# 32-column tiles and attention in fewer, larger visits, in a fused Linformer attention and hard-swish MLP

## The chip, the cores and the metric

One Trainium2 chip, one of its cores. The metric is the device time of one execution in microseconds (us). Every quoted time is a median of single executions; their range stands beside it where it matters.

## The reference

Eight batches of eight heads, 1024 tokens, head size 64. Keys and values are projected along the sequence to 64 rows (E and F), so that attention is over 64 keys. Its output is the input of an MLP with a hard-swish gate.

```python
k_proj = einsum('ks,bhsd->bhkd', E, k);  v_proj = einsum('ks,bhsd->bhkd', F, v)
scores = q @ k_proj.T / sqrt(64)
attn = softmax(scores)                      # over the 64 projected keys
x = (attn @ v_proj)  -> (8 * 1024, 512)     # heads side by side
h = x @ w_in                                # 512 -> 2048
out = (h * clip(h + 3, 0, 6) / 6) @ w_out   # 2048 -> 512, float32
```

## The kernel before

The MLP of a batch is two halves of 512 tokens. A half has 16 *first groups* (a row block of h: 4 blocks of the 512 inputs summed in one PSUM bank, then the gate on ScalarE and VectorE) and 4 *output groups* (16 blocks summed in one bank, then a copy and a write to DRAM). The output groups of one half run between the first groups of the next, one after every four. Attention of the next batch is done at those places in *visits*: TensorE leaves the MLP for a few matmuls of another tile shape. A change of shape leaves a gap between matmuls, called a *drain* here. Two pools of four PSUM banks each, `mm` and `at`, go round in order; a bank comes free when ScalarE or VectorE has read it out (its *eviction*).

Parts that the change touches (cuts marked):

```python
    ps_mm = ctx.enter_context(tc.tile_pool(name="ps_mm", bufs=4, space=bass.MemoryType.PSUM))
    ps_at = ctx.enter_context(tc.tile_pool(name="ps_at", bufs=4, space=bass.MemoryType.PSUM))
    width = [P // 2]                      # 64 columns of the array per matmul

    def in_columns(ps, stationary, moving, **flags):
        for lo in range(0, stationary.shape[-1], width[0]):
            nc.tensor.matmul(ps[lo:lo + width[0]], stationary[:, lo:lo + width[0]], moving, **flags)
    # ... cut ...
        def all_sums(self, alloc):        # denominators of all heads: 128x32 tiles
            tiles = [alloc() for _ in range(2)]
            for h in range(H):
                j, a, c = h // 2, h % 2, h % 4
                nc.tensor.matmul(tiles[h // 4][32 * c:32 * c + 32].rearrange("p (r n) -> p r n", r=2),
                                 halves.rearrange("p t i -> p (t i)"), self.aT[j][:, :, a, :],
                                 start=True, stop=True)
            return tiles

        def spread(self, den):            # reciprocals to DRAM and back, one row to 64 partitions
            few = att.tile([P, 2, TOK], f32, tag="few", name="few", bufs=1)
            inverse(few, den)             # two logarithms, one exponential on ScalarE
            rows = dram.tile([H, NB, TOK], f32, tag="rows", name="rows")
            nc.sync.dma_start(out=rows..., in_=few[::16])
            self.recs = [rec_tile() for _ in range(KO)]
            for h in range(H):
                nc.sync.dma_start(out=self.recs[h // 2]..., in_=rows[h:h + 1]...to_broadcast([D, NB * TOK]))
    # ... cut: visit(n), the four visits of batches 1 and 2, each head pair's sums made with 64x64 tiles ...
            if b == 1:                    # batch 2 is attended here, by head pair
                n -= SB
                if n < 3:
                    return lambda: second.visit(n, third), nothing
                return nothing, lambda: second.visit(n, third)()
            if b + 1 < B:                 # batches 3 to 7: several visits, sums and first values together
                # ... cut: two special scores visits and a projection of batch 2 ...
                if n == 0:
                    return nothing, lambda: second.some_scores((1, 2, 3), ((pmm, pmm), (pat, pat), (pat, pmm)), third)
                if n == 2:
                    return second.sums_and_values, nothing
                if n == 5:
                    return second.first_products, nothing
                if n == 6:
                    return lambda: second.last_values(third), nothing
    # ... cut ...
        for t in range(NB):
            if b == 1 and t == 1:
                qT_dma[3] = q_transposed(3)     # transposing DMA, SyncE's queue
```

The softmax here doesn't subtract the row's maximum and nothing guards it: scores larger than these inputs give would overflow.

## Time and profile before

| | before |
|---|---|
| time, median of 6 executions | 507.19 us (507.05 to 507.40) |
| span in the profile | 505.5 us |
| TensorE busy, mean granted clock | 99%, 1.0 |
| matmuls; runs of one tile shape | 4858; 92 |

TensorE is the bound, so what counts is any time in which it does not start the next *set* of tiles (the matmuls that share the array side by side: two of 64 columns or four of 32). I read that from the *starts* of matmuls in the timeline, because the ends are modelled; the prediction below shows the lines. In them `few` are the logarithms and reciprocals of the sums, `rows` their copy in DRAM, `rec` the broadcast reciprocals, `xT` the output of the attention, `r` and `g` the gate. Two more page lines of before are of use later, the products of the values with the reciprocals (they wait for ScalarE, never for a DMA) and the queue of instruction fetches (count, MB, share):

```profile
q8 instruction: 38, 0.62, 0.5%
L264 DVE TENSOR_TENSOR xT<-at,rec 128x512 bf16<-128x512 f32 x42 | 26.5, 681 | 6.5 <-ACT rec L184 6.5
```

### The profile page before, as it was taken

How to read it: one execution, taken by the hardware profiler on the slowest of the kernel's cores; microseconds unless marked ns; L12 is line 12 of the kernel's file. 1: busy time of each engine (PE TensorE's matmuls, PEld its weight loads, DVE VectorE, ACT ScalarE, POOL GpSimd, SP SyncE). 2: the span in 40 equal slices, each digit the busy share in tenths (PEclk: the TensorE clock that was granted, in tenths of full speed). 3: DMA queues.
4: the chain of work that ended last, by engine and by line, in shares of the span. 5: the costliest groups of instructions: out<-in, count | busy, mean ns of one | idle time of the engine just before them, and what ended most of it. 6: DMA issues, size and time to landing. Idle time of an engine off the chain costs nothing.

```text
span 505.5 us, 11242 instructions
## 1 busy us (share of the span) xinstructions
PE 498.9 (99%) x4858; PEld 259.5 (51%) x4858; DVE 245.1 (48%) x384; ACT 256.1 (51%) x438; POOL 38.7 (8%) x58
## 2 busy tenths in 40 slices
PE   8999999999999999999999999999999999999997
PEld 4554554554454555545554555545555555555554
DVE  3572736865733564536635455533752446334420
ACT  3757466566565444653555544654455544344431
POOL 8620020020020020020001000000000000000000
PEclk9999999999999999999999999999999999999999
DMA  9999979799299999699416992248110361101112
GB/s 168 198 205 208 200 131 231 142 155 202 73 151 194 230 169 190 137 154 249 123 43 118 205 249 69 61 100 209 43 43 29 82 164 43 39 26 43 43 43 84
DMA packets 78074, 66.30 MB, mean 131 GB/s; under 512 B 36216, under 2 KB 67192, under 8 KB 78024
## 3 DMA queue, kind: packets, MB, share of 16 engines
q0 software_dynamic: 32480, 29.36, 37.4%
q1 hardware_dynamic: 45320, 35.89, 27.7%
q8 instruction: 38, 0.62, 0.5%
q10 hardware_dynamic: 224, 0.33, 0.2%
q14 instruction: 12, 0.10, 0.1%
HBM read 69.73 MB, written 16.94 MB: 171 GB/s over the span
## 4 chain that ended last, share of the span: by engine, by line
PE 85%; DMA 12%; POOL 2%; ACT 1%; issue 0%; DVE 0%; ACTq 0%; POOLq 0%
PE mm L172 79%; DMA q<-in_q_dram 6%; DMA w_in_sb<-in_moe_w_in_dram 2%; PE at L172 2%; DMA v<-in_v_dram 2%; DMA qT<-q 2%; PE at L251 1%; PE at L233 1%; PE mm L251 1%; POOL q L106 1%; PE mm L271 1%; POOL k L110 1%; ACT aT L242 0%; PE mm L233 0%; POOL v L110 0%
## 5 line engine op out<-in xcount | busy, mean ns | idle before, releaser
L512 DVE SCALAR_TENSOR_TENSOR g<-r,mm 128x512 bf16<-128x512 f32 x256 | 173.5, 686 | 178.7 <-ACT r L511 177.9
L172 PE MATMUL mm<-w_out_sb,g 128*64 128x512 bf16 (+2 forms) x2080 | 235.0, 376 | 0.2 <-DVE g L512 0.2
L172 PE MATMUL mm<-xT,w_in_sb 128*64 128x512 bf16 x2048 | 231.5, 379 | 0.3
L511 ACT ACTIVATE r<-mm 128x512 f32<-128x512 f32 x256 | 152.2, 599 | 74.5 <-PE mm L172 73.5
L172 PEld LDWEIGHTS <-w_in_sb 128*64 128x64 bf16 x2048 | 117.2, 110 | 104.0 <-issue 0.8
L172 PEld LDWEIGHTS <-g 128*64 128x64 bf16 x2080 | 116.2, 110 | 105.5 <-issue 7.0
L546 ACT COPY o_sb<-mm 128x512 f32<-128x512 f32 x55 | 32.2, 586 | 126.7 <-PE mm L172 126.7
L264 DVE TENSOR_TENSOR xT<-at,rec 128x512 bf16<-128x512 f32 x42 | 26.5, 681 | 6.5 <-ACT rec L184 6.5
L242 ACT ACTIVATE aT<-at 128x512 bf16<-128x512 f32 x38 | 20.2, 615 | 9.1 <-PE at L233 9.1
L208 DVE CAST kp<-at 64x512 bf16<-64x512 f32 x12 | 7.7, 677 | 15.9 <-PE at L172 15.9
L223 POOL COPY mark<-qT 1x1 bf16<-1x1 bf16 x4 | 0.7, 176 | 165.0 <-DMA qT<-q 165.0
L242 ACT ACTIVATE aT<-mm 128x512 bf16<-128x512 f32 x18 | 10.3, 613 | 3.9 <-PE mm L233 3.9
L546 DVE COPY o_sb<-mm 128x512 f32<-128x512 f32 x8 | 5.5, 687 | 13.8 <-PE mm L172 13.8
L172 PE MATMUL at<-v,f_t 128*64 128x512 bf16 x48 | 11.4, 381 | 0.3 <-DMA v<-in_v_dram 0.3
L172 PE MATMUL at<-k,e_t 128*64 128x512 bf16 x48 | 11.6, 382 | 0.0
L264 DVE TENSOR_TENSOR xT<-mm,rec 128x512 bf16<-128x512 f32 x14 | 9.0, 685 | 4.3 <-PE mm L251 4.3
L184 ACT ACTIVATE rec<-rec 128x1024 f32<-128x1024 f32 x10 | 10.6, 1060 | 0.3
L178 ACT ACTIVATE rec<-mm 128x512 f32<-128x512 f32 x10 | 5.5, 595 | 7.9 <-PE mm L251 5.4
L178 ACT ACTIVATE few<-mm 128x512 f32<-128x512 f32 x10 | 5.4, 594 | 7.4 <-PE mm L271 7.4
L93 PE MATMUL mm<-ones 128*128 128x512 bf16 x18 | 7.4, 549 | 1.5 <-DVE halves L84 1.5
L172 PEld LDWEIGHTS <-e_t 128*64 128x64 bf16 x56 | 5.7, 110 | 6.0 <-issue 1.8
L211 DVE CAST vp<-at 64x512 bf16<-64x512 f32 x12 | 8.3, 694 | 0.4
(73 smaller groups left out, 155.0 us busy)
## 6 DMA issues: line engine op xcount, KB each, us to landing
out_dram<-o_sb SPq DMA_DIRECT2D x63, 256.0 KB, 3.0
rec<-rows SPq DMA_DIRECT2D x40, 256.0 KB, 6.5
k<-in_k_dram POOLq DMA_DIRECT2D x7, 1024.0 KB, 15.0
v<-in_v_dram POOLq DMA_DIRECT2D x7, 1024.0 KB, 20.7
q<-in_q_dram POOLq DMA_DIRECT2D x7, 1024.0 KB, 10.0
w_out_sb<-in_moe_w_out_dram POOLq DMA_DIRECT2D x4, 512.0 KB, 16.0
w_in_sb<-in_moe_w_in_dram POOLq DMA_DIRECT2D x5, 256.0 KB, 9.7
k<-in_k_dram POOLq DMA_DIRECT2D x4, 256.0 KB, 5.5
```

The costliest lines, as they stand in the source:

```text
L93: nc.tensor.matmul(ps, ones[:, :P], ones, start=True, stop=True)
L172: nc.tensor.matmul(ps[lo:lo + width[0]], stationary[:, lo:lo + width[0]], moving, **flags)
L178: nc.scalar.activation(rec[:, i], den, AF.Ln)
L184: nc.scalar.activation(flat, flat, AF.Exp, scale=-1.0)
L208: nc.vector.tensor_copy(self.kp[:, :, a, :], self.ps[:KP].rearrange("p (h d) -> p h d", d=D))
L211: nc.vector.tensor_copy(self.vp[a * KP:(a + 1) * KP], self.ps[KP:].rearrange("p (h d) -> p h d", d=D))
L242: nc.scalar.activation(self.aT[j][:, r].rearrange("p a n -> p (a n)"), tiles[r], AF.Exp, scale=scale)
L251: nc.tensor.matmul(tiles[t][c:c + D].rearrange("p (r n) -> p r n", r=2), stationary(r, 2 * j + a), self.aT[j][r:r + KP, :, a, :], start=Tr ...
L264: nc.vector.tensor_mul(self.xT[:, j, t, :], av[t], rec[:, t])
L511: nc.scalar.activation(r, h_ps, AF.Relu, bias=0.5, scale=1.0 / 6.0)
L512: nc.vector.scalar_tensor_tensor(g[:, fo, :], r, 1.0, h_ps, op0=ALU.min, op1=ALU.mult)
L546: (copy or nc.scalar.copy)(o_sb, o_ps)
```

## The change

Its intent: let the big matmuls use the same tile shape, 128x32, as the sums of the softmax, so that the sums no longer drain TensorE; and collect the attention of a batch into few visits that use all eight banks, to change shape less often. Batch 2, until now attended by head pair with its sums kept on the chip, gets the same treatment: its reciprocals go out to DRAM and are broadcast back. The diff cut to its core:

```diff
+    width[0] = P // 4                     # from batch 1 on: four matmuls instead of two
+        def all_banks(self, make, take):
+            tiles = [make(j, *two) for j, two in enumerate(((pmm, pmm), (pat, pat), (pat, pat), (pmm, pmm)))]
+            for j in (0, 3, 1, 2):        # two head pairs evicted now, two spread over later groups
+                take(j, tiles[j], later.append if j in (1, 2) else lambda f: f())
 # ... cut ...
-            if b == 1: ... return lambda: second.visit(n, third), nothing   # and the rest of visits()
+        inside, behind_it = {}, {}
+        if b == 1:
+            behind_it = {4: second.all_scores, 5: second.sums_spread}
+            inside = {6: second.first_values, 7: second.last_values}
+        elif b == 2:
+            inside = {0: second.projected}
+            behind_it = {1: second.all_scores, 2: second.sums_spread, 4: third.projected, 6: second.all_values}
+        elif b + 1 < B:
+            behind_it = {0: second.all_scores, 1: second.sums_spread, 5: second.all_values}
+            if third:
+                behind_it[3] = third.projected
 # ... cut ...
-                rows = second_group(*behind[0], fo // SB, nc.vector.tensor_copy if b == 1 else None)
+                rows = second_group(*behind[0], fo // SB,
+                                    nc.vector.tensor_copy if (b, n) in ((1, 4), (2, 1)) or (b > 2 and n == 0) else None)
```

`inside` runs in the middle of an output group, `behind_it` after it. The numbers are output groups of the half behind, 0 to 7 within a batch. The transposing DMA of batch 3's queries stays where it was. Cut, but part of the change: batch 1's first scores visit comes four blocks (8 matmuls) later, the projections move, and the queries of batches 5 to 7 are loaded after their keys and values and no longer before them.

More of the change, by code (lines that the diff above doesn't have):

```diff
@@ L223, in turn @@
                 nc.gpsimd.tensor_copy(mark, last)
-                load_kqv(self.b + 1, "kvq" if self.b in (1, 3) else "qkv")
+                load_kqv(self.b + 1, "qkv" if self.b == 2 else "kvq")
         def scores(self, j, *allocs):
@@ L237, in scores, with exps @@
             return tiles
-        def exps(self, j, tiles):
-            self.aT[j] = att.tile([P, 2, 2, HT], bf16, tag="aT", name="aT", bufs=KO + 1)
+        def exps(self, j, tiles, when=lambda f: f()):
+            self.aT[j] = aT = att.tile([P, 2, 2, HT], bf16, tag="aT", name="aT", bufs=KO + 1)
             for r in range(2):
-                nc.scalar.activation(self.aT[j][:, r].rearrange("p a n -> p (a n)"), tiles[r],
-                                     AF.Exp, scale=scale)
+                when(lambda r=r: nc.scalar.activation(aT[:, r].rearrange("p a n -> p (a n)"), tiles[r],
+                                                      AF.Exp, scale=scale))
         def quads(self, stationary, j, allocs):
@@ L260, in values, with scaled @@
             return self.quads(lambda r, h: self.vp[r:r + KP, h, :], j, allocs)
-        def scaled(self, j, av, rec):
+        def scaled(self, j, av, rec, when=lambda f: f()):
             for t in range(NB):
-                nc.vector.tensor_mul(self.xT[:, j, t, :], av[t], rec[:, t])
+                when(lambda t=t: nc.vector.tensor_mul(self.xT[:, j, t, :], av[t], rec[:, t]))
         def all_sums(self, alloc):
@@ L285, in spread, with projected, all_scores, all_values @@
                                   in_=rows[h:h + 1].rearrange("h t n -> h (t n)").to_broadcast([D, NB * TOK]))
-        def projected(self, alloc=pat):
-            self.project(alloc)
+        def projected(self):
+            self.project(pat)
             self.keys_out()
-            rest = [lambda: self.values_out(0), lambda: None, lambda: None, lambda: self.values_out(1)]
-            if alloc == pmm:
-                for r in rest:
-                    r()
-                rest = []
-            later.extend([self.turn] + rest)
-        def some_scores(self, js, allocs, following=None):
-            tiles = [self.scores(j, *alloc) for j, alloc in zip(js, allocs)]
-            for j, two in zip(js, tiles):
-                self.exps(j, two)
-            if following:
-                following.projected()
-        def sums_and_values(self):
-            den = self.all_sums(pmm)
+            later.extend([self.turn, lambda: self.values_out(0), lambda: None,
+                          lambda: self.values_out(1)])
+        def all_banks(self, make, take):
+            tiles = [make(j, *two) for j, two in enumerate(((pmm, pmm), (pat, pat), (pat, pat), (pmm, pmm)))]
+            for j in (0, 3, 1, 2):
+                take(j, tiles[j], later.append if j in (1, 2) else lambda f: f())
+        def all_scores(self):
+            self.all_banks(self.scores, self.exps)
+        def all_values(self):
+            self.all_banks(self.values, lambda j, av, when: self.scaled(j, av, self.recs[j], when))
+        def sums_spread(self):
+            self.spread(self.all_sums(pmm))
+        def first_values(self):
             self.av = [self.values(j, pat, pat) for j in range(2)]
-            self.spread(den)
         def first_products(self):
@@ L314, in first_products, with last_values, visit @@
                 self.scaled(j, self.av[j], self.recs[j])
-        def last_values(self, following):
-            av = [self.values(2, pmm, pmm), self.values(3, pat, pat)]
-            if following:
-                following.some_scores((0,), ((pat, pat),))
+        def last_values(self):
+            av = [self.values(2, pmm, pmm), self.values(3, pmm, pat)]
             for i in range(2):
                 self.scaled(2 + i, av[i], self.recs[2 + i])
-        def visit(self, n, following):
+        def visit(self, n):
             if n == 0:
-                self.some_scores((2, 0, 1), ((pmm, pmm), (pat, pat), (pat, pat)))
+                js = 2, 0, 1
+                tiles = [self.scores(j, *two) for j, two in zip(js, ((pmm, pmm), (pat, pat), (pat, pat)))]
+                for j, two in zip(js, tiles):
+                    self.exps(j, two)
                 return lambda: None
@@ L348, in visit @@
             self.scaled(2, early, self.rec)
-            if following:
-                following.project(pat)
-                later.extend([following.turn] + [lambda a=a: following.values_out(a) for a in range(2)])
-            def rest():
-                self.scaled(3, av, rec)
-                if following:
-                    following.keys_out()
-            return rest
+            return lambda: self.scaled(3, av, rec)
     class First:
@@ L622 @@
             pop()
-            if i == 0:
-                rest.append(second.visit(c, None))
+            if i == (c == 0):
+                rest.append(second.visit(c))
             elif i == 2 or c == SB - 1:
@@ L637 @@
         third = Attention(b + 2) if b + 2 < B else None
-        def visits(b, n):
-            def nothing():
-                pass
-            if b == 1:
-                n -= SB
-                if n < 3:
-                    return lambda: second.visit(n, third), nothing
-                return nothing, lambda: second.visit(n, third)()
-            if b + 1 < B:
-                six = (pmm, pmm), (pat, pat), (pat, pat)
-                if (b, n) == (2, 0):
-                    return lambda: second.some_scores((2, 0, 1), six), nothing
-                if (b, n) == (2, 1):
-                    return lambda: second.some_scores((3,), six[1:2]), nothing
-                if (b, n) == (2, 3):
-                    return lambda: third.projected(pmm), nothing
-                if n == 0:
-                    return nothing, lambda: second.some_scores(
-                        (1, 2, 3), ((pmm, pmm), (pat, pat), (pat, pmm)), third)
-                if n == 2:
-                    return second.sums_and_values, nothing
-                if n == 5:
-                    return second.first_products, nothing
-                if n == 6:
-                    return lambda: second.last_values(third), nothing
-            return nothing, nothing
+        inside, behind_it = {}, {}
[9 more added lines that the diff above has]
+                behind_it[3] = third.projected
         for t in range(NB):
@@ L683 @@
                     continue
-                inside, after = visits(b, t * SB + fo // SB)
-                rows = second_group(*behind[0], fo // SB, nc.vector.tensor_copy if b == 1 else None)
+                n = t * SB + fo // SB
+                if (b, n) == (1, 7):
+                    second.first_products()
+                rows = second_group(*behind[0], fo // SB,
+                                    nc.vector.tensor_copy if (b, n) in ((1, 4), (2, 1)) or (b > 2 and n == 0) else None)
                 next(rows)
                 next(rows)
-                rest = inside()
+                if n in inside:
+                    inside[n]()
                 whole(rows)
-                after()
-                if rest:
-                    rest()
+                if n in behind_it:
+                    behind_it[n]()
             behind = [(b, t, g)]
```

## The prediction

> **What bounds the kernel now.** I read the page first, then the timeline of TensorE in stretches of batches 2 to 6, then the timelines of all engines around the attention visits, then the DMA issues of SyncE. The page says that TensorE is the bound: busy 99%, its clock at full speed in every slice, and the chain that ended last is almost wholly its matmuls.
>
> ```profile
> PE 498.9 (99%) x4858; PEld 259.5 (51%) x4858; DVE 245.1 (48%) x384; ACT 256.1 (51%) x438; POOL 38.7 (8%) x58
> PEclk9999999999999999999999999999999999999999
> ```
>
> A busy engine can still lose time between matmuls, so I looked at starts. In the timeline (start us, duration us, engine, line) 32 matmuls of 64 columns, that is 16 pairs, take 207.48 to 210.93:
>
> ```profile
> 207.48 3.62 PE L172 MATMUL mm<-w_out_sb,g 128*64 128x512 bf16 x32
> 210.93 3.62 PE L172 MATMUL mm<-xT,w_in_sb 128*64 128x512 bf16 x32
> 214.38 1.89 PE L172 MATMUL mm<-w_out_sb,g 128*64 128x512 bf16 x16
> 216.21 0.61 PE L271 MATMUL mm<-aT,halves 128*32 128x512 bf16 x8
> 216.75 0.63 PE L251 MATMUL at<-aT,vp 64*64 64x512 bf16 x8
> 217.31 1.05 PE L172 MATMUL mm<-w_out_sb,g 128*64 128x512 bf16 x8
> ```
>
> That is 3.45/16 = 0.216 us a pair, against 512 columns at 2.4 GHz = 0.213. The stream is within 1.3% of its floor. What is left is **changes of tile shape**: the 8 pairs from 214.38 take 1.83 us instead of 1.73, the 8 sums of 128x32 (two sets of four) 0.54 instead of 0.43, the 8 of 64x64 0.56 instead of 0.43: about 0.12 us at each change. Before has, by its instruction order, 92 runs of one shape.
>
> **What the Trainium skill says.** (1) "TensorEngine Tiling (Array Packing)", Key Properties: changing the tiling mode drains TensorE, changing the tile within a mode does not. The trace agrees: 0.12 us at each change. (2) The same page, PSUM Bottleneck: tiling speeds up TensorE but not the emptying of PSUM, which may become the bound. The stall at 382 below is such a case. (3) "TensorE: Matmul & The Clock Gate", Back-to-back issue gap: a warm matmul of 512 columns costs 512/2.4 plus some 2.5 ns. The trace's 0.216 agrees; I take the 2.5 ns to be per set of tiles side by side, as pairs show. (4) The same page, Part 1: after about 3.4 us of idleness the clock falls to half. The only stop shown here is at the very end of the trace, so no stretch of the kernel before tests it.
>
> **The change, part by part.**
>
> *32-column tiles.* Some 1870 sets of two become sets of four: twice the matmuls and weight loads in the same 0.216 us, so 8 instructions in 216 ns. The scores already do more: 24 matmuls and 24 loads from 106.07 to 106.85. And the sums show that four tiles of 128 rows stream at once: their two sets take 0.54 with the change of shape in it. So the stream itself: 0 us. Its use is that the sums (128x32) no longer change the shape.
>
> ```profile
> 106.07 0.41 PE L233 MATMUL mm<-qT,kT 64*64 64x256 bf16 x8
> 106.31 0.61 PE L233 MATMUL at<-qT,kT 64*64 64x256 bf16 x16
> 106.85 1.92 PE L172 MATMUL mm<-w_out_sb,g 128*64 128x512 bf16 x16
> ```
>
> *Fewer visits.* The instruction order of after has 74 runs of one shape: 18 changes fewer x 0.12 = **-2.2 us**. Batch 2's sums by head, 4 sets of 0.216 where the new form needs 2: **-0.4**. Stalls that go: 0.27 before the first scores at 68.80 (a transposing DMA; the visit moves half a microsecond or more later), some 0.3 at 139, and 0.66 after the scores of the last attended batch at 382, where three evictions on ScalarE precede what TensorE waits for: **-1.2**.
>
> *All eight banks in one visit.* The four banks of mm and four of at go round in order, so a visit that takes four mm tiles takes the bank of the output just summed, too, and the groups after it meet its evictions. The stall at 382 of before gives the delays:
>
> ```profile
> 381.49 0.41 PE L233 MATMUL mm<-qT,kT 64*64 64x256 bf16 x8
> 381.60 0.58 ACT L546 COPY o_sb<-mm 128x512 f32<-128x512 f32 x1 [2.86 <-PE mm L172]
> 382.26 3.97 PE L172 MATMUL mm<-xT,w_in_sb 128*64 128x512 bf16 x32
> 384.95 2.14 ACT L511 ACTIVATE r<-mm 128x512 f32<-128x512 f32 x4
> 385.65 2.48 DVE L512 SCALAR_TENSOR_TENSOR g<-r,mm 128x512 bf16<-128x512 f32 x4 [6.19 <-ACT r L511]
> 386.39 3.64 PE L172 MATMUL mm<-w_out_sb,g 128*64 128x512 bf16 x32 [0.16 <-DVE g L512]
> ```
>
> The copy of an output starts 0.11 after the next matmul; from a group's activation to the release of its bank is 386.39 - 384.95 = 1.44.
> Scores visit, from its first matmul S: three heads' pairs end at S+0.68; the eighth bank is that of the output, whose copy (now VectorE, 0.69) ends at S+0.11+0.69+0.05 = S+0.85: 0.17 of stall, six visits = **+1.0**. The later evictions fit: the exponentials are spread over the following groups.
> Sums visit, from its first matmul E: no drain, so the copy starts at E+0.21; then two logarithms (0.54 each) and an exponential of 1.06 end near E+2.85; the first activation of the next groups comes only then, its bank is free at E+2.82+1.44 = E+4.26. The output group that wants this bank is due at E+0.44+16x0.216 = E+3.90: 0.36, six visits = **+2.2**. In before half of an output group lay behind the sums and hid this.
> Values visit: the first product (0.69) starts 0.45 after the visit's start and frees the next group's bank at 1.19, due at 1.05; with 0.06 for the eighth bank 0.19, five visits = **+1.0**.
>
> *Batch 2's sums through DRAM.* This is the term that decides. By the same rates batch 1 in after has its sums at 115.7, their exponential done near 118.6. The reciprocals then go out and come back through SyncE's queue, behind the transposing DMA of batch 3's queries, which is unchanged:
>
> ```profile
> 110.73 13.55 SPq L160 DMA_TRANSPOSE qT<-q  x1
> 124.37 8.00 SPq L547 DMA_DIRECT2D out_dram<-o_sb  x4
> 157.13 0.72 SPq L281 DMA_DIRECT2D rows<-few  x1
> 160.50 4.96 SPq L284 DMA_DIRECT2D rec<-rows  x8
> ```
>
> It holds SyncE until 124.3 because the loads of batch 3's keys and values fill the DMA engines until about 123.6. Then two output writes (0.6, 0.4) stand before the rows: issued at 125.3, landed behind the outputs at about 128.2. Eight broadcasts follow: by before's semaphore records the first lands 3.7 us after its issue (160.50, 164.16), then one each 1.14 us (the last at 172.0). So 131.9, 133.0, ... 139.9. Two make one pair of heads. The products then stand at: first pair 133.05 to 134.4, second from 135.35, third from 137.6, fourth from 139.9 to 140.6 for its first half.
> TensorE comes to the last values of batch 2 at 129.3; their eighth tile needs the at bank of the first product: waits till 133.8. Half an output group, 1.73, to 135.85. Batch 2's first two groups need xT of pair 2 (136.0), pair 3 (138.35), pair 4 (140.65) and end at 141.1. Without waiting they end at 133.3: **+7.8 us**. TensorE being the bound, nothing later gives it back. A pause of some 4 us may drop the clock (the skill's fourth point): half speed for one to two microseconds of what follows, an expected **+0.7**.
>
> Sum: 507.3 - 2.2 - 0.4 - 1.2 + 1.0 + 2.2 + 1.0 + 7.8 + 0.7 = **516.2**; I say 516.
>
> **The rivals.** *A: the reciprocals come in time.* If the queries' transposing DMA lets SyncE go at about its usual 4.9 us (as at 92.6, 266.9 and 326.9 in before), the rows go out at 118.6 and the last broadcast lands near 132: a stall of at most 1 us, total 508 to 509. Against it: nothing in the change touches that DMA or the loads it competes with. *B: the new visits don't stall,* because the schedule was laid out for it (copies on VectorE, exponentials deferred): then the recurring 4.2 us vanish, 512 with the batch 2 stall, 504 with A as well. Against it: the bank order and the stall at 382, which the same arithmetic reproduces. *C: 32-column tiles stream worse* (loads of weights not hidden, or the sequencer at its limit): each 5 ns a set costs 9 us. Against it the scores and the sums above; for it, that no long stream of such sets is in the trace. *D: the clock falls at the pause and stays low* for its whole window or more: 1 to 2 us on top, 518.
>
> **Range and chances.** A at about 15%, B in part 20%, C 8%, D 25% of the cases. 80% range 507 to 519. Faster by over 2% (below 497.2) needs a gain that no term holds: 3%. Slower by over 2% (above 517.5) comes with C, D or a longer wait in batch 2: 24%. The rest, 73%, within 2%.
>
> **What would show the steps right or wrong.** A pause of TensorE of 3 to 5 us near 129, and two smaller ones before 141, ended by VectorE's products, which themselves waited on DMA rec<-rows; the rows issued after 124 and behind the queries' transposing DMA. Steady sets of four each 0.216 us. After each sums visit from batch 2 on, the next output group started about 0.4 us late, released by VectorE g; after scores and values visits 0.2. 74 runs of one shape, 0.12 us at each change. The prediction is wrong if the rows go out before 120, if sets of four are spaced by more than 0.218 us, or if the first values of batch 2 find their reciprocals landed.

## The result, and the profile after

| | before | after |
|---|---|---|
| time, median of 6 | 507.19 us | 518.73 us (517.14 to 519.56) |
| span in the profile | 505.5 us | 516.9 us |
| mean granted clock | 1.0 | 0.993 |
| runs of one tile shape | 92 | 74 |

The ratio of fast runs is 1.0223 (95% interval 1.0209 to 1.0238). It is, here and below, the mean time of one kernel's fast runs over the mean of the other's in the same rounds, so it is not quite the ratio of the medians quoted. The kernel is slower by just over 2%.

These page lines answer to those of before: TensorE's busy share fell to 97%; one slice of the clock row (the eleventh, 129 to 142 us) is a 7; the products now wait 7.5 us for `rec<-rows`, a DMA, and matmuls wait 6.4 us for a product; instruction fetches rose from 38 to 67.

```profile
PE 501.5 (97%) x8562; PEld 269.2 (52%) x8562; DVE 245.8 (48%) x387; ACT 243.6 (47%) x426; POOL 38.7 (7%) x58
PEclk9999999999799999999999999999999999999999
q8 instruction: 67, 1.10, 0.9%
L264 DVE TENSOR_TENSOR xT<-at,rec 128x512 bf16<-128x512 f32 x31 | 20.8, 684 | 13.3 <-DMA rec<-rows 7.5
L251 PE MATMUL at<-aT,vp 64*64 64x512 bf16 x62 | 5.5, 385 | 6.4 <-DVE xT L264 6.4
```

**The stage between batches 1 and 2.** The table of fixed windows says where the loss is. First before, then after; columns are the window, its length, busy time and instruction count of each engine, then the granted clock, the DMA share and GB/s:

```profile
127.00:146.00 19.00, 18.99 (x196) 9.60 (x194) 12.32 (x19) 12.41 (x22) 2.80 (x4) 1.00 0.39 70
```

```profile
127.00:146.00 19.00, 12.25 (x175) 5.12 (x170) 9.01 (x14) 4.06 (x7) 0.00 (x0) 0.82 0.79 178
```

TensorE is idle for 6.75 us of these 19, and the clock averages 0.82. The timeline of SyncE in after tells why (start, duration, issuing instruction):

```profile
112.93 13.35 SPq L160 DMA_TRANSPOSE qT<-q  x1
126.38 1.94 SPq L541 DMA_DIRECT2D out_dram<-o_sb  x2
128.41 0.72 SPq L281 DMA_DIRECT2D rows<-few  x1
131.52 4.96 SPq L284 DMA_DIRECT2D rec<-rows  x8
```

The transposing DMA of batch 3's queries holds SyncE from 112.93 to 126.28. Two output writes, then the reciprocals stand behind it. By the semaphore records the eight broadcasts land from 135.09 to 142.96. And the timeline of TensorE and VectorE there:

```profile
130.59 0.62 PE L251 MATMUL mm<-aT,vp 64*64 64x512 bf16 x6
136.86 1.29 DVE L264 TENSOR_TENSOR xT<-at,rec 128x512 bf16<-128x512 f32 x2 [6.55 <-DMA rec<-rows]
137.60 0.64 PE L251 MATMUL at<-aT,vp 64*64 64x512 bf16 x2 [6.39 <-DVE xT L264]
138.17 3.61 PE L172 MATMUL mm<-w_out_sb,g 128*32 128x512 bf16 x32
141.39 1.29 DVE L264 TENSOR_TENSOR xT<-mm,rec 128x512 bf16<-128x512 f32 x2 [0.98 <-DMA rec<-rows]
142.13 4.03 PE L172 MATMUL mm<-xT,w_in_sb 128*32 128x512 bf16 x64 [0.36 <-DVE xT L264]
143.08 0.69 DVE L264 TENSOR_TENSOR xT<-mm,rec 128x512 bf16<-128x512 f32 x1 [0.40 <-DMA rec<-rows]
145.98 1.91 PE L172 MATMUL mm<-w_out_sb,g 128*32 128x512 bf16 x32
```

The values visit stops after six of its eight matmuls, because the seventh needs a bank that a product must empty, and the product needs its reciprocals. It waits 6.39 us. The next eight sets (32 matmuls) then start 427 ns apart, not 216: the record of the granted clock stands at 0.5 from 136.1 to 142.9. The stage's excess over an undisturbed one is 9.6 us: 7.0 in the visit and 2.6 from there to the end of batch 2's first four groups at 145.98. The half clock makes eight sets 1.7 us longer, but that is no loss of its own: they stand ahead of a wait. The matmul at 142.13 could not start before the product of 141.39, nor the seventh set of these groups (143.82 in the trace) before the product of 143.08, and both products waited for broadcasts, the last of which landed at 142.96. So the last landing sets the end of the stage; the experiment with a busy pause comes back to this.

**The recurring visits.** A sums visit of after, on all engines:

```profile
280.00 0.60 PE L271 MATMUL mm<-aT,halves 128*32 128x512 bf16 x8
280.43 3.63 PE L172 MATMUL mm<-xT,w_in_sb 128*32 128x512 bf16 x64
280.70 1.09 ACT L178 ACTIVATE few<-mm 128x512 f32<-128x512 f32 x2
281.83 1.06 ACT L184 ACTIVATE few<-few 128x1024 f32<-128x1024 f32 x1
282.79 2.04 ACT L505 ACTIVATE r<-mm 128x512 f32<-128x512 f32 x4
284.14 1.05 PE L172 MATMUL mm<-w_out_sb,g 128*32 128x512 bf16 x16
```

The sums take 0.43 us, exactly two sets: no drain. But the four first groups behind them take 284.14 - 280.43 = 3.71 us instead of 3.45, since their first gate starts only at 282.79, behind the logarithms and the exponential. So 0.26 us are lost. Scores and values visits show 0.20 us of excess beyond their shape changes.

**Outside all this**, the first wait for batch 1's values near 55 us was 1.3 us longer in this execution, in a part of the program that the change leaves as it was; over the traces of all kernels here that wait varies from nothing to 1.8 us. And from the end of the last copy to the end of the program it takes 3.23 us instead of 2.65.

### The profile page after: what moved, and what is told of

Same layout as the page of the kernel before. It is cut to its first block, busy times and chain, and to the rows that moved or that the text cites. A ratio compares the mean times of both kernels' runs of the same rounds, so it can differ in the third digit from the quotient of the medians.

```text
span 516.9 us, 18651 instructions
## 1 busy us (share of the span) xinstructions
PE 501.5 (97%) x8562; PEld 269.2 (52%) x8562; DVE 245.8 (48%) x387; ACT 243.6 (47%) x426; POOL 38.7 (7%) x58
## 4 chain that ended last, share of the span: by engine, by line
PE 82%; DMA 11%; ACT 2%; issue 2%; POOL 1%; DVE 1%; SPq 1%; ACTq 0%; DVEq 0%; POOLq 0%
PE mm L172 76%; DMA v<-in_v_dram 7%; PE at L172 2%; DMA w_in_sb<-in_moe_w_in_dram 2%; DMA rec<-rows 1%; ACT few L178 1%; PE mm L233 1%; PE mm L251 1%; PE at L251 1%; DVE g L506 1%; PE at L233 1%; ACT r L505 1%; DMA rows<-few 1%; POOL q L106 1%; SPq L284 1%
## 5 line engine op out<-in xcount | busy, mean ns | idle before, releaser
L172 PE MATMUL mm<-w_out_sb,g 128*32 128x512 bf16 (+3 forms) x3904 | 235.1, 378 | 0.4
L172 PE MATMUL mm<-xT,w_in_sb 128*32 128x512 bf16 (+1 forms) x3840 | 232.8, 380 | 0.6 <-DVE xT L264 0.4
L172 PEld LDWEIGHTS <-g 128*32 128x32 bf16 (+1 forms) x3904 | 122.1, 98 | 102.1 <-issue 6.7
L172 PEld LDWEIGHTS <-w_in_sb 128*32 128x32 bf16 (+1 forms) x3840 | 119.2, 98 | 102.9 <-issue 4.9
L264 DVE TENSOR_TENSOR xT<-at,rec 128x512 bf16<-128x512 f32 x31 | 20.8, 684 | 13.3 <-DMA rec<-rows 7.5
L264 DVE TENSOR_TENSOR xT<-mm,rec 128x512 bf16<-128x512 f32 x25 | 15.7, 684 | 14.2 <-PE mm L251 12.9
L172 PE MATMUL at<-v,f_t 128*32 128x512 bf16 (+1 forms) x104 | 13.2, 379 | 1.6 <-DMA v<-in_v_dram 1.6
L172 PE MATMUL at<-k,e_t 128*32 128x512 bf16 (+1 forms) x104 | 13.5, 379 | 0.0
L172 PEld LDWEIGHTS <-e_t 128*32 128x32 bf16 (+1 forms) x104 | 6.2, 98 | 6.9 <-issue 2.1
L233 PEld LDWEIGHTS <-kT 64*64 64x64 bf16 x224 | 5.7, 106 | 4.2 <-issue 4.1
## 6 DMA issues: line engine op xcount, KB each, us to landing
w_out_sb<-in_moe_w_out_dram POOLq DMA_DIRECT2D x4, 512.0 KB, 15.9
```

The costliest lines, as they stand in the source:

```text
L233: nc.tensor.matmul(tiles[r][t * KP:(t + 1) * KP, a * HT:(a + 1) * HT], self.kT[r * D:(r + 1) * D, 2 * j + a, :], qT[r * D:(r + 1) * D, j, ...
L264: when(lambda t=t: nc.vector.tensor_mul(self.xT[:, j, t, :], av[t], rec[:, t]))
```

## The experiments

The theory after reading the traces: (1) the greater part of the loss (9.6 of 11.4 us between the two traces) is batch 2's reciprocals, late because they queue behind a transposing DMA on SyncE; (2) the new visits return what the saved shape changes bring; (3) sets of four cost nothing in the stream. Rivals: 32-column tiles are slow in themselves; or the detour through DRAM is slow even when it is issued in time.

### Batch 3's queries after batch 2's reciprocals

After, with one DMA issued later:

```diff
-            if b == 1 and t == 1:
-                qT_dma[3] = q_transposed(3)
 # ...
                 if n in behind_it:
                     behind_it[n]()
+                if (b, n) == (1, 5):
+                    qT_dma[3] = q_transposed(3)
```

> The changed kernel with one thing moved: the transposing DMA of batch 3's queries is issued behind the eight broadcasts of batch 2's reciprocals and not before them. Theory (SyncE's queue, held by that DMA, is what makes the reciprocals late): the rows go out near 120 and not at 128.4, the last broadcast lands some 6 us earlier, the long pause in the last values visit of batch 2 (6.4 us in the changed kernel) is gone, some 3 to 4 us of waiting for the last pairs' reciprocals before batch 2's first group stay, the clock stays at full speed: 512 to 514 us. Rival (the DMA engines' bandwidth under the loads of batch 3 is the limit, whatever the order): the broadcasts land as late as before, 517 us or more.

Measured: 511.62 us (510.88 to 512.02), just under the range that I expected; ratio to before 1.0082 (1.0069 to 1.0095). SyncE in this run:

```profile
118.51 0.71 SPq L281 DMA_DIRECT2D rows<-few  x1
123.02 4.96 SPq L284 DMA_DIRECT2D rec<-rows  x8
128.15 9.14 SPq L160 DMA_TRANSPOSE qT<-q  x1
```

and TensorE:

```profile
129.16 0.62 PE L251 MATMUL mm<-aT,vp 64*64 64x512 bf16 x6
129.53 0.40 PE L251 MATMUL at<-aT,vp 64*64 64x512 bf16 x2
129.86 1.91 PE L172 MATMUL mm<-w_out_sb,g 128*32 128x512 bf16 x32
133.35 1.48 PE L172 MATMUL mm<-xT,w_in_sb 128*32 128x512 bf16 x24 [1.58 <-DVE xT L264]
136.71 2.34 PE L172 MATMUL mm<-xT,w_in_sb 128*32 128x512 bf16 x40 [1.88 <-DVE xT L264]
```

The values visit no longer stops, and the clock stays at full speed. The medians differ by 7.1 us for moving one DMA. Between the two traces it is 6.7: 5.7 in this stage (an excess of 3.9 and not 9.6) and 1.4 from the early wait, which was short here, less 0.4 of a longer tail. So the order on SyncE's queue is shown to be the cause of 5.7 to 7.1 us of the loss, half of it or more. The last broadcast lands 7.1 us earlier (135.88 against 142.96), so it was not the load of the DMA engines alone. The two waits left, some 3.8 us by starts, come from the broadcasts themselves, which land one every 1.3 us up to 135.88: even issued in time, the way through DRAM takes from 118.5 to 135.9.

### Batch 2 by head pair, as before

After, with batch 2's four visits of the kernel before and the projection behind the fourth (cut: VectorE again copies all outputs of that stretch, as in before):

```diff
-            behind_it = {4: second.all_scores, 5: second.sums_spread}
-            inside = {6: second.first_values, 7: second.last_values}
+            inside = {4 + i: lambda i=i, a=second: a.visit(i) for i in range(3)}
+            behind_it = {7: lambda a=second, f=third: a.visit(3, f)()}
```

> The changed kernel with batch 2 attended as in the kernel before (four visits, sums by head, no trip through DRAM, keys and values of batch 3 projected behind the fourth). Theory: the pause and the half clock, together 9.6 us in the trace, go; two more changes of tile shape and 0.4 of sums come back, 0.5 of stalls in batch 2's scores and sums visits go: 509.0 to 509.8 us. Rival (the recurring visits or the 32-column stream are the greater part of the loss): 513 or more.

Measured: 507.68 us, ratio 1.0013 (0.9998 to 1.0027): lower than I expected, in part because there was no early wait for values in its trace (1.8 us less than in after). With batch 2 taken back, 11 of the 11.5 us are gone. Everything else in the change, 32 columns, fewer visits and their new stalls, comes out at nothing within 0.3%.

### 32 columns alone, on the kernel before

```diff
+    width[0] = P // 4
     second = Attention(2)
```

> The kernel before with 32-column tiles from batch 1 on and nothing else. It has 88 runs of one tile shape where before has 92. Theory (a set of four streams as a pair does, a change of shape costs 0.12 us): 0.5 us faster, 506.7, ratio 0.999. Rival (weights or instructions of four tiles are not hidden): each 1 ns a set costs 1.9 us, so over 508 us.

Measured: 509.85 us (508.56 to 512.56), ratio 1.0052 (1.0033 to 1.0071). My theory said 506.7 and was wrong, yet the stream was as I said: steady sets of four start 216 ns apart. The loss sits in one place, the projection of batch 5:

```profile
202.56 0.39 PE L172 MATMUL at<-k,e_t 128*32 128x512 bf16 x2
204.78 0.39 PE L172 MATMUL at<-v,f_t 128*32 128x512 bf16 x2 [1.82 <-DMA v<-in_v_dram]
```

The values landed at 204.73 here, at 201.53 in before, where they were due at 202.3: before had a margin of 0.8 us. Some 2.0 us are lost to that wait and 0.6 in the tail (3.21 us against 2.65). The load was issued 3.3 us later, too (184.18 against 180.91), and so it was in the eased pair below (183.73 with 32 columns, 180.81 with 64): the shift comes with the tiles, but what makes it is not shown.

### 64 columns in the changed kernel

After without `width[0] = P // 4`.

> The changed kernel with 64-column tiles throughout. It has 85 runs of one tile shape where the changed kernel has 74. Theory: 11 changes of 0.12 us more, 1.3 us slower than the changed kernel of the same rounds, about 520. If the sums visit's drain gives ScalarE time, 0.1 a visit less. Rival (32 columns cost the stream something): as fast as the changed kernel or faster.

Measured: 515.30 us (514.48 to 515.40), ratio 1.0152 (1.0139 to 1.0165). That is 3.4 us *faster* than after, where I expected 1.3 slower. By the traces (its profiled execution was its fastest, 514.48): 2.1 us less in the stage between batches 1 and 2, 1.1 in the early wait for values (jitter), 0.6 in the tail, and no loss at the sums visits:

```profile
276.47 0.62 PE L271 MATMUL mm<-aT,halves 128*32 128x512 bf16 x8
277.01 3.64 PE L172 MATMUL mm<-xT,w_in_sb 128*64 128x512 bf16 x32
280.50 3.64 PE L172 MATMUL mm<-w_out_sb,g 128*64 128x512 bf16 x32
```

The sums now take 0.54 us, and the sets ahead of them another 0.1, for the two drains; but the groups behind take 3.49, not 3.71. The evictions still end when they end: the drain is spent inside the wait. This is the part of the change that I had counted as pure gain. Under a following wait, saving the drain was worth nothing. The 2.1 us are the reciprocals again: their rows went out at 124.81 and not 128.41, the transposing DMA having let SyncE go at 123.61 and not 126.28, in both traces 0.7 to 0.8 us after batch 3's values had landed. Why these landed 2.7 us earlier, by chance or by the tiles, is open.

### Batch 2 by head pair, sums in the middle of an output group

The kernel of the second experiment, and for batches 3 to 7 the sums moved so that half an output group lies behind them, as before had it:

```diff
-            behind_it = {0: second.all_scores, 1: second.sums_spread, 5: second.all_values}
+            behind_it = {0: second.all_scores, 5: second.all_values}
+            inside = {2: second.sums_spread}
# ... cut: the same for batch 3, in output group 3 ...
```

> The changed kernel with batch 2 by head (as the run that took 507.68) and, for batches 3 to 7, the sums visit moved from behind an output group into the middle of the next one (a sums visit changes no tile shape with 32 columns). Theory: the stall of 0.263 us at the output group after each of the five sums visits goes, since half an output group lies between the sums and the next activations: 1.3 us less, 506.2 to 506.5 us, under the kernel before. Rival (ScalarE's work is only moved and another group waits): 507.5 as without.

Measured: 506.80 us, ratio 0.9989 (0.9976 to 1.0001), a little over what I expected. The 0.26 us behind each sums visit are gone in its trace. That the stall comes from the work of ScalarE close behind the sums, as the prediction had it, is thereby confirmed; on the clock the gain over the second experiment is likely and not settled, since the two intervals overlap.

### TensorE kept busy in the pause

After, with 24 matmuls on constants inside the last values visit, to keep the clock up.

> The changed kernel with 24 matmuls of ones (128x128, their result overwritten) in the last values visit of batch 2, ahead of the wait for the first product: 5.2 of the 6.4 us of pause are filled with useless work. Theory: the clock stays at full speed, so the sets of the next output group take 0.216 and not 0.427 us: 8 x 0.21 = 1.7 us less, some of it given back to the reciprocals that are waited for anyway (the last two pairs land when they land): 517.0 to 518.5, and granted clock 1.00 throughout in the trace. Rival (the half clock cost nothing, all of it lay in time that is waited for anyway): 518.7 as the changed kernel.

Measured: 517.66 us, ratio 1.0211 (1.0195 to 1.0227). The time lies in the range that I expected, but not for my reason. The clock still fell, only later: 0.5 from 140.1 to 143.5, after the next wait (2.31 us from 138.0 on), and seven or eight sets ran at half speed all the same. Of the gain of 1.1 us, 0.6 is a shorter tail.

```profile
140.31 5.20 PE L173 MATMUL mm<-xT,w_in_sb 128*32 128x512 bf16 x64 [2.31 <-DVE xT L265]
```

The output group ahead of that wait ran at full speed here, and TensorE then waited 2.31 us in place of 0.36: the half clock had only filled the wait. What the stage's end follows is the last broadcast. It landed at 142.96 in after, at 139.31 in after with 64 columns and at 135.88 in the first experiment, and batch 2's first four groups ended 3.0 us later each time (145.98, 142.34, 138.86), with half clock before it in the first two and none in the third. Here it landed at 141.62 and they ended at 145.33, 3.7 us later. So the half clock cost after nothing, as this run's rival said, and about 0.7 us here, where the groups behind the last landing ran into it.

### The kernel before with its tight places eased, in both widths

Before, with the first scores visit 8 matmuls later, the output copied by VectorE ahead of two scores visits, and the projection of batch 5 one output group later; once with 64 columns, once with 32.

```diff
-                        (1, 2, 3), ((pmm, pmm), (pat, pat), (pat, pmm)), third)
+                        (1, 2, 3), ((pmm, pmm), (pat, pat), (pat, pmm)), third if b != 3 else None)
+                if (b, n) == (3, 1):
+                    return nothing, third.projected
```

> The kernel before with three small things: batch 1's first scores visit 8 matmuls later, VectorE and not ScalarE copies the output ahead of the scores visits of batches 4 and 7 (6 and 3 in the loop's count), and the projection of batch 5 one output group later, so that its values have 7 us more to land. 64 columns. Theory: 0.27 and some 0.5 us of stalls gone, 0.15 come: 506.5 to 506.8 us.

> The same as the run before it with 32 columns from batch 1 on. In the run of the kernel before with 32 columns alone the trace shows 2.0 us of waiting for batch 5's values in their projection, whose landing came 3 us later than in before; here that projection has 7 us of slack. Theory (32 columns cost nothing in the stream and 4 changes of shape go; the loss came only from that transfer): 0.5 us under its twin with 64 columns, 506.1. Rival (32 columns cost time in the stream itself): 2 us or more above the twin.

Measured: 64 columns 507.77 us, ratio 1.0007 (0.9994 to 1.0019), so my easing brought nothing (the scores visits of batches 4 and 7, with no projection behind them, stall 0.5 us). 32 columns 508.04, ratio 1.0015 (1.0002 to 1.0027): the 2 us wait of the third experiment is gone, so that loss was a shifted schedule and not the tiles. But the expected gain over the twin did not show. The last copy ended 0.7 us earlier than in the twin (502.48 against 503.16), and the tail was 0.9 longer (3.51 against 2.62).

### Pairs again in the last two output groups

Every trace with 32 columns to the end but one (that of the busy pause) has a long tail, 3.06 to 3.58 us, and every trace with 64 a short one, 2.57 to 2.65. With twice the matmuls there are 67 instruction fetches of 16,384 bytes, each about 1 us; in after one starts at 513.5, and the last copy ends at 513.68, so that the last output is written while it is under way. In before the last one, 500.3 to 501.3, is over when the last copy ends at 502.84. To test this, the best kernel so far got 64 columns in its last two output groups, and, in the other kernel, throughout:

```diff
     for c in range(SB):
+        if c == SB - 2:
+            width[0] = P // 2
         whole(second_group(*behind[0], c))
```

> The best version so far (batch 2 by head, sums inside an output group, 506.8 us) with the last two output groups on 64-column tiles: 190 TensorE instructions fewer, one change of tile shape more. In all traces with 32 columns but one the program ends 3.06 to 3.58 us after the last copy, with 64 columns 2.57 to 2.65; in the 32-column ones an instruction fetch of 16 KB starts 0.1 to 0.5 us before that copy ends, in the exception (2.59) 1.0 us before. Theory (the fetch holds a DMA engine that the last output needs): with no fetch in the last microseconds the tail is 2.6 us, 0.4 us less in sum: 506.2 to 506.5. Rival (the tail comes from something else that 32 columns do): the tail stays above 3 us.

> The best version so far on 64-column tiles throughout. Its instruction order has 85 runs of one tile shape instead of 76, since each sums visit changes the shape twice. Theory: 9 changes of 0.12 us more = 1.1, the tail 0.5 less: 0.5 to 0.7 us slower than with 32 columns, 507.3 to 507.5. Rival (32 columns cost time in the stream or in the transfers): as fast or faster.

Measured: 505.85 us (505.55 to 506.41), ratio 0.9972 (0.9959 to 0.9986), and 506.99 us with 64 columns throughout, ratio 0.9994 (0.9982 to 1.0007), both some 0.3 us under what I expected. With equal tails (2.65 and 2.63 us) 32 columns are worth 1.1 us: five sums visits with two drains of about 0.12 each, 1.2. Then the tail, in the same rounds:

> The same kernel as e6_both (sets of four to the end), run in the same rounds as its twin with pairs in the last two output groups, since the two were timed in different calls. If the last output is held back by an instruction fetch that falls just before the end, the stretch from the last copy's end to the program's end is 3.1 us or more here and about 2.65 in the twin, and this kernel is 0.4 to 0.9 us slower than the twin. Rival: the 0.95 us between the two calls was jitter of the early load of batch 1's values; then the two agree within 0.2 us and the tails differ no more than by chance.

> The twin with pairs of 64 columns in the last two output groups. Fetch theory: 505.8 to 506.3 us, tail 2.6 to 2.7 us, 0.4 to 0.9 faster than the twin of the same rounds. Jitter theory: within 0.2 us of it.

Measured: 506.78 us with sets of four to the end, 506.18 with pairs there (ratios 0.9986 and 0.9981, with intervals of about 0.0013 either way). In the traces, tails of 3.46 and 2.63 us; the last fetches started at 501.9 and 496.5. The tail follows the fetch as expected. The 0.6 us between the medians is of the expected size, but at five runs each the two ratios' intervals overlap, so on the clock it is likely and not settled; the run with a busy pause fits, since its last fetch was over (512.0 to 513.0) when the last copy ended, and its tail is 2.59. As it has 32 columns to the end, it is the one trace that separates the fetch from the tiles.

With 0.2 to 0.3% below the kernel before in two calls, this version beats both kernels; the margin over before is some 1.2 us.

## Why the prediction was right, and where it was not

The time, 518.73, lies inside the range of 507 to 519, near its upper end; within 2% was called the likeliest, and the result passed that line by 1.2 us, into the case that was given 24%. Step by step:

| term | predicted | in the trace |
|---|---|---|
| 18 fewer shape changes | -2.2 | 74 runs, 0.12 us a change: as predicted |
| batch 2's sums | -0.4 | half the sets, by construction |
| stalls that go | -1.2 | those at 68.80 and 382 gone; the one near 139 had been 0.18, not 0.3 |
| scores visits | +1.0 | 6 x 0.20 = 1.2 |
| sums visits | +2.2 | 6 x 0.26 = 1.6 |
| values visits | +1.0 | 5 x 0.20 = 1.0 |
| batch 2's reciprocals, waits | +7.8 | 9.6 |
| half clock | +0.7 | nothing of its own (it lay within the waits) |
| tail of the program | not seen | +0.6 |
| early wait for values | not seen | +1.3 in the profiled run, jitter |

**The term that decides was right in cause, and 1.8 us too small.** The reciprocals stood behind the transposing DMA, and the first experiment shows that this order is the cause. The broadcasts came 3.1 us later than worked out (the last at 142.96 against 139.9), TensorE itself 1.3 (130.59 against 129.3); the rest is the 1.8. The waits were distributed otherwise than told, one of 6.4 us and a small one and not three of middle size, since the half clock filled what would have been the second. That the sum came within 2.5 us is in part luck: this term and the tail were too small, the half clock and the sums visits too large. Rival A, reciprocals in time, fell.

**The half clock came, but its cost did not** (rival D, "1 to 2 us on top"). The clock stood at 0.5 for 6.8 us after a pause of 6.4, and eight sets took twice their time. The error was to add this to waits that end when a broadcast lands: TensorE, at either speed, had to wait for the last one. That D's 518 is near the result is luck.

**The sums visit was mis-sized** by 0.1 each: the chain of evictions was right (last activation behind the logarithms, the bank order), its delays a little too long. Rival B fell: all visits stall. What I had not seen is that this stall *contains* the drain which the 32 columns save, so in after their gain at the sums did not arrive. The run with 64 columns in the changed kernel shows it at the visit.

**Rival C, that sets of four stream worse, fell**: 680 matmuls in 37.08 us with one sums stall of 0.27 in them, 36.81 without it, which is 216.5 ns a set. But 32 columns do cost in a way that I had not thought of: 67 blocks of instructions are fetched in place of 38, and in the traces where the last fetch falls beside the last output, the tail is 0.4 to 0.9 us longer. And without any slowness of their own they can shift a schedule with 0.8 us of margin into a 2 us wait (third experiment).

**Still open**: how much of the 1.3 us of early wait is in after's median and not only in its profiled run; and why batch 3's values land 2.7 us earlier in the trace of after with 64 columns, which shortens its stage between batches 1 and 2 by 2.1 us.

## What to carry to other kernels

Before sums or scales are sent through DRAM, look at what already stands in that queue: a long transposing DMA ahead of them made a 17 us way (118.5 to 135.9) into one of 23 us (119.9 to 143.0), and issuing it behind the broadcasts gave back 7 of 11.5 us (5.7 in that stage, by the traces). Before a slow clock or a slow matmul is counted as a loss, look at what ends the stage: where the next step waits for a DMA anyway, it costs nothing. A saved drain or a saved shape change is worth something only where no eviction ends the same wait; move the visit so that half a group of work lies behind it, and only then count the gain. After doubling the instruction count, look at the tail of the program as well as at the stream.

## What the Trainium skill lacked or had wrong

- "TensorEngine Tiling (Array Packing)", Key Properties, names the drain at a change of mode but gives no time: 0.10 to 0.12 us a change here. It also doesn't say that a set of four 128x32 tiles streams as densely as a pair: 216.5 ns a set.
- The same page, PSUM Bottleneck, warns that emptying PSUM may bound. It lacks the consequence shown here: a drain of 0.24 us removed in front of a wait of 0.26 saves nothing until the wait is gone (1.1 us over five visits after that).
- "Runtime: NRT & Kernel Launch", Instruction fetch mechanics, says that instructions come in 16 KiB blocks and that crossing one is mostly hidden. The trace agrees on 16,384 bytes (about 1 us each), and in the stream none was seen to stop TensorE. At the end it seems not to be hidden: tails of 3.46 against 2.63 us in the traces with and without one beside the last output.
- "TensorE: Matmul & The Clock Gate", Part 1, has the idle window of about 3.4 us and the half clock. After's trace agrees (0.5 from 136.1 to 142.9 after a wait of 6.4 us), and so does the first experiment's (none after waits of 1.6 and 1.9). The run with a busy pause does not: there the clock fell at 140.1 after a wait of 2.31 us, with matmuls until 138.0. So less than a whole idle window was enough.
